# Which squares wait in DRAM: batches of plain-float32 matmuls every 32 steps, and every 48

## The chip, the core and the metric

The kernel runs on one core of a Trainium2 chip. The time is the device time of one execution in microseconds (us). Before the change it is 2217.09 us, the median of three runs (2216.71 to 2217.1). TensorE (PE) multiplies matrices, VectorE (DVE) and ScalarE (ACT) do elementwise work and take results out of PSUM, GpSimd (POOL) adds, and SyncE (SP) and ScalarE start DMAs.

## What is computed

A causal convolution of 7 softmaxed taps over 32,768 tokens of 192 features, then a two-layer network with a squared ReLU between:

```python
w = softmax(weight)                                  # 8 heads x 7 taps
x = einsum('hk,bskhg->bshg', w, unfolded(x))         # 32768 tokens x 192 features
h = x @ w_in                                         # 192 -> 2048
r = np.maximum(h, 0.0)
g = s * (r * r) + b
out = g @ w_out                                      # 2048 -> 192
```

Everything is float32. Most matmuls are done on pairs of a rounded part and a low part; that for the output's last 64 features is not.

## The kernel before, in words

Tokens lie along the free dimension. A **super** is 1024 tokens, `n` counts the 32 of them; a **block** is half of it (`j`, 512 tokens). The 2048 hidden features come in 8 pairs `p` of 128 + 128. A **step** is one (n, j, p): `first` (L528) makes 18 matmuls of the first layer into the PSUM tile `h`; ScalarE takes ReLU (L556) and square (L564) into a room `q`; VectorE rounds it to `qh` (L566) and takes the low part `ql` (L570); and two steps later `second` (L724) adds 12 matmuls into the accumulators of output features A, the first 128.

**Features B**, the last 64, aren't done in the step. From super 2 on (`OLD = 2`) the float32 squares are kept, and `second_B` (L743) multiplies them plainly, a whole block at a time: 64 matmuls on two PSUM banks, `acc1` and `acc2`. `banks()` hands these out of a pool with two of each name, so that block i of a batch writes the banks that block i - 2 had. `evict_B` takes the two banks out on ScalarE (L755, L756), adds them on GpSimd (L757), moves half of the rows by a DMA (L758), adds again (L761) and sends the result (L762).

The squares are kept in a ring of 12 rooms (`RING`), each of 1 MB for two steps, hence 24 steps. A batch is run at every 32nd step. Of a batch's four blocks, the first eight steps' squares have been sent to DRAM (`send`, L581, one DMA of 1 MB for every two steps, on SP's queue) and are called back (`call_back`, L591, four DMAs of 1 MB on ScalarE's queue) into rooms that the batch itself empties. So each batch has three **near** blocks, whose squares are in the ring, and one **far** block, done last. A room is given out when its last reader is done, so a call-back waits for a pair of matmul groups of the batch.

What sets the order: within PE, VectorE and ScalarE the instructions stay in the order in which the code is written (`in_order`), the DMAs that ScalarE starts among them. The convolution's taps (VectorE, L181 and L183, seven to a block's half) are handed out in pieces by `convolve(k)`: 7 pieces at the edge of a round, 5 during each block of a batch (`WINDOW`), none in the six steps from an edge on, then one or two in a step (`pace`). After the taps of the last 64 features, ScalarE rounds (L215) and starts the next input's load `xB` (L173). Each DMA counts its landing on one of eight shared counters, given out in turn; one that gets a counter again waits until the DMA that had it has landed.

Of the kernel before, what the change touches and what calls it, by code (L numbers as in the profile page):

```python
# [9 lines left out]
F32 = mybir.dt.float32  # L10
# [7 lines left out]
P = 128  # L18
BLK = 512
# [9 lines left out]

RING = 12  # L30

BATCH = 32

WINDOW = (5, 5, 5, 5)


GAP = 40

OLD = 2
# [9 lines left out]
def conv_attention_then_squared_relu_mlp(  # L49
# [23 lines left out]
    nc = tc.nc  # L73
    D, T = outT.shape
    NPAIR = weights64.shape[0]
# [28 lines left out]
    far = ctx.enter_context(tc.tile_pool(name="far", bufs=2, space=bass.MemoryType.DRAM))  # L104
    late = ctx.enter_context(tc.tile_pool(name="late", bufs=1))
    sumB = late.tile([P, 3 * DB], F32, name="sumB")
    ps_h = ctx.enter_context(tc.tile_pool(name="ps_h", bufs=2, space=bass.MemoryType.PSUM))
# [20 lines left out]
    @contextmanager  # L128
    def in_order(*engines):

        traced = nc.cur_bb.bb.instructions
        start = len(traced)
        yield
        for e in engines:
            mine = [i for i in traced[start:] if i.engine == e.engine]
            for before, i in zip(mine, mine[1:]):
                tc.add_manual_dep(
                    i,
                    before.name,
                    mybir.DependencyInfo(  # L140
                        mybir.DependencyClass.NoSync, mybir.DependencyReason.DATA
                    ),
                    reason="in_order",
                )
# [201 lines left out]
    def room_for(dtype):  # L346
        return act.tile([P, 2, 2, BLK], dtype, name="q")

    def flat(room):
        return room.rearrange("p a b c -> p (a b c)")  # L350

    places = [flat(room_for(I32)) for _ in range(3)]
    raw, rest = flat(room_for(I32)), flat(room_for(I32))
# [188 lines left out]
    two = [None]  # L542
# [16 lines left out]
    def squares(h, cast):  # L559
        return square(relu(h), cast)  # L560
# [8 lines left out]
    def lows(q, qh, ql):  # L569
        nc.vector.tensor_tensor(ql, q, qh.bitcast(F32), op=ALU.subtract)  # L570
        return qh, ql

    kept = {}

    away, double = {}, {}

    def send(n, p, queue=nc.sync):

        if p == 1:
            away[n] = far.tile([P, NPAIR // 2, 4 * BLK], F32, name="away")  # L580
        queue.dma_start(  # L581
            away[n][:, p // 2], double[n, p].rearrange("p a b c -> p (a b c)")
        )
        for k in (p - 1, p):
            del kept[n, 0, k]

    def call_back(n):

        for k in range(NPAIR // 2):
            room = room_for(F32)  # L590
            nc.scalar.dma_start(room.rearrange("p a b c -> p (a b c)"), away[n][:, k])  # L591
            for i in range(2):
                kept[n, 0, 2 * k + i] = room[:, i]
        del away[n]

    def put(n, j, p, pair):
        if n >= OLD:
            kept[n, j, p] = pair[0]
            if j == 0 and n % 2 == 0 and p % 2:
                double[n, p] = two[0]  # L600
        queue.append((n, j, p, *lows(*pair)))

    acc = {}
# [1 line left out]
    def banks():  # L605
        return [ps_o.tile([P, BLK], F32, name=f"acc{k}") for k in (1, 2)]
# [7 lines left out]
    room = ("oA", "oB", "oC", "oB2", "oA2", "oC2")  # L614

    def out_tile(name):
        return outs[:, room.index(name), :]
# [119 lines left out]
    def second_B(n, j, accs):  # L737

        for p in range(NPAIR):
            q = kept.pop((n, j, p))  # L740
            for r in (slice(0, HB), slice(HB, P)):
                for i in range(2):
                    nc.tensor.matmul(  # L743
                        accs[r.start // HB][i * DB : (i + 1) * DB], WB[r, p, i, :], q[r, i, :],
                        start=p == 0, stop=p == NPAIR - 1, skip_group_check=True,
                    )
        return accs

    def evict_B(n, j, accs, turn=0):

        t0 = n * SUP + j * BLK
        rooms = (("oB", "oB2", "oC"), ("oA", "oA2", "oC2"))[turn]
        o, o2, oC = (out_tile(name) for name in rooms)
        oC = oC[0:DB]
        nc.scalar.activation(o, accs[0], AF.Identity, scale=sb, bias=bias[:, 1:2])  # L755
        nc.scalar.activation(o2, accs[1], AF.Identity, scale=sb)  # L756
        nc.gpsimd.tensor_tensor(o, o, o2, op=ALU.add)  # L757
        nc.sync.dma_start(oC, o[DB:P])  # L758

        def rest():  # L760
            nc.gpsimd.tensor_tensor(oC, oC, o[0:DB], op=ALU.add)  # L761
            nc.sync.dma_start(outT[P:D, t0 : t0 + BLK], oC)  # L762

        return rest

    def last_B(n, j, accs):

        t0 = n * SUP + j * BLK
        oB = out_tile("oC2")[0:DB]
        nc.scalar.activation(  # L770
            oB, accs[0][DB:P], AF.Identity, scale=sb[DB:P], bias=bias[DB:P, 1:2]
        )
        for a in (accs[0][0:DB], accs[1][0:DB], accs[1][DB:P]):
            nc.vector.scalar_tensor_tensor(oB, a, sb[0:DB], oB, op0=ALU.mult, op1=ALU.add)
        nc.sync.dma_start(outT[P:D, t0 : t0 + BLK], oB)
# [20 lines left out]
    queue = []  # L796

    now = [0]
# [55 lines left out]
    def convolve(k):  # L854

        k += owed[0]
        owed[0] = 0
        while k > 0:
            said = next(stream, "over")
            if said in ("over", "gated"):  # L860
                return
            k -= 1
            burst[0] = k > 0
            if said == "tapped":
                owed[0] = k
                return
# [42 lines left out]

    def batch(k):  # L910

        n = OLD + 2 * k - 2
        rest = []
        for block, parts in zip(((n, 1), (n + 1, 0), (n + 1, 1), (n, 0)), WINDOW):
            a = second_B(*block, banks())
            convolve(parts)
            with in_order(nc.gpsimd, nc.sync):
                rest.append(evict_B(*block, a, len(rest) % 2))
                if len(rest) > 1:
                    rest[-2]()  # L920
            if block == (n + 1, 1):
                send(n + 2, 1, nc.scalar)
        convolve(0)
        rest[-1]()

    def pace(g):
        return 0 if g % BATCH < 6 else 2 if g % BATCH in (18, 20, 22) else 1

    steps = [(n, j, p) for n in range(NSUP) for j in range(2) for p in range(NPAIR)]

# [2 lines left out]
    def step(n, j, p):  # L933
        now[0] = 16 * n + 8 * j + p
        if p == 0:
            if j == 0:
                need(n, "A", 0)
                need(n, "B", 0)
                tok.pop(n - 1)
            else:  # L940
                need(n, "A", 1)
        g = now[0] - 16 * OLD
        h = first(n, j, p)
        edge = g % BATCH if g >= BATCH else BATCH
        if edge == 0:
            convolve(4)
            convolve(3)
            second(*queue.pop(0))
            waiting.append((n, j, p, h))
            return  # L950
        if edge == 1:
            second(*queue.pop(0))
            *at, before = waiting.pop()
            put(*at, squares(before, nc.vector.tensor_copy))
        put(n, j, p, squares(h, nc.scalar.copy if n == OLD and p % 2 else nc.vector.tensor_copy))
        if edge == 1:
            call_back(n - 2)
        if (n, j) == (1, 1):
            if p < NPAIR - 1:
                column_sums(p + 1)  # L960
            convolve(1)
        elif n <= OLD:
            convolve(3 if n == 1 else 2)
        else:
            convolve(pace(g))
        if (n, j, p) == (2, 0, 0):
            biases()
        elif n == 2 and p % 2 == 0 and unbiased:
            add_bias()
        if (n, j, p) == steps[-1]:  # L970
            call_back(n - 1)
            a = second_B(n - 1, 1, banks())
            evict_B(n - 1, 1, a)()
            for k, block in enumerate(((n, 0), (n - 1, 0), (n, 1))):
                h = ps_h.tile([P, 2, BLK], F32, name="h")
                a = second_B(*block, [h[:, k, :] for k in range(2)])
                if block == (n, 1):
                    last_B(*block, a)
                else:
                    evict_B(*block, a, 1 - k)()  # L980
            for item in queue:
                second(*item)
        while queue and len(queue) > LAG + (
            queue[0][2] == 0 and queue[0][0] <= OLD and queue[0][:2] not in ((1, 0), (OLD, 1))
        ):
            if (n, j, p) == steps[-1]:
                break
            second(*queue.pop(0))
        if edge == 1:
            batch(g // BATCH)  # L990
        sent = now[0] - 1
        if n >= OLD and sent % 32 < 8 and sent % 2 and edge != 2:
            send(sent // 16, sent % 8)

    with in_order(nc.vector, nc.scalar, nc.tensor):
        with in_order(nc.sync):
# [60 lines left out]
```

## Time and profile before

| What | us |
|---|---|
| Median of 3 runs | 2217.09 |
| The profiled execution | 2217.3 |
| Its span on the core | 2215.5 |
| Busy: PE, VectorE, ScalarE, GpSimd | 2210.2, 1610.6, 1331.4, 273.3 |
| Moved by DMA | 243.32 MB, mean 110 GB/s |
| From one batch to the next (410.50 to 547.19 in the chain) | 136.69 |

The span is the time from the first to the last instruction in the trace; 1.8 us of the execution lie around it. Fourteen batches of four blocks stand within the steps and one at the end, 60 blocks in all.

### The profile page before, as it was taken

To read this page: it belongs to the slowest core of one execution; us is meant where nothing else is said; L and a number is where in the kernel's file an instruction comes from. 1 tells how busy PE (TensorE), PEld (TensorE's weight loads), DVE (VectorE), ACT (ScalarE), POOL (GpSimd) and SP (SyncE) were. 2 spreads that over 40 slices of the span, in tenths; PEclk is the share of its full clock that TensorE was granted. 3 is DMA by queue.
4 is the path that set the end of the run, shared out by engine and by line. 5 is a ranking of instruction groups with operands and counts; after the bars stand their busy time and mean duration, and the time that the engine had idled before them with its cause. 6 is when DMAs were issued, how large, how long until landed. Compare 5 with 4: busy or idle time off the path is not lost.

```text
span 2215.5 us, 44748 instructions
## 1 busy us (share of the span) xinstructions
PE 2210.2 (100%) x19334; PEld 1611.2 (73%) x19334; DVE 1610.6 (73%) x1859; ACT 1331.4 (60%) x1449; POOL 273.3 (12%) x199
## 2 busy tenths in 40 slices
PE   9999999999999999999999999999999999999999
PEld 6788768587685876858778586785867858678585
DVE  8888777777777777777767777676776767767662
ACT  8759656466564665646556465564656646566463
POOL 0011020100202002020020201202011020110201
PEclk9999999999999999999999999999999999999999
DMA  5114151422515224152341523315233152421512
GB/s 167 39 32 161 55 199 53 162 91 65 193 49 162 100 77 173 54 172 82 104 144 54 174 86 117 126 53 191 73 132 107 54 195 68 146 94 53 205 30 103
DMA packets 63285, 243.32 MB, mean 110 GB/s; under 512 B 9648, under 2 KB 9904, under 8 KB 47728
## 3 DMA queue, kind: packets, MB, share of 16 engines
q1 hardware_dynamic: 43648, 138.98, 19.9%
q10 hardware_dynamic: 19440, 101.49, 12.9%
q8 instruction: 151, 2.47, 0.5%
q14 instruction: 46, 0.38, 0.1%
HBM read 94.55 MB, written 88.08 MB: 82 GB/s over the span
## 4 chain that ended last, share of the span: by engine, by line
PE 98%; DVE 1%; DMA 0%; ACT 0%; issue 0%; SPq 0%; DVEq 0%; ACTq 0%
PE h L528 47%; PE acc L724 29%; PE acc L743 18%; PE acc L670 2%; PE h L743 1%; PE acc L640 0%; PE acc L646 0%; DVE acc L183 0%; PE acc L648 0%; PE acc L647 0%; DVE ql L570 0%; PE acc L639 0%; DMA xA<-in_xA 0%; PE acc L642 0%; DVE q L308 0%; DVE q L322 0%
## 5 line engine op out<-in xcount | busy, mean ns | idle before, releaser
L556 ACT ACTIVATE q<-h 128x1024 f32<-128x1024 f32 x512 | 525.7, 1027 | 502.4 <-PE h L528 487.0
L566 DVE CAST qh<-q 128x1024 fp32r<-128x1024 f32 x482 | 334.1, 693 | 484.9 <-ACT q L564 481.6
L570 DVE TENSOR_TENSOR ql<-q,qh 128x1024 fp32r<-128x1024 f32 x498 | 623.8, 1253 | 56.4 <-ACT qh L566 4.9
L724 PE MATMUL acc<-qh,W 64*128 64x512 f32 x3816 | 588.0, 386 | 0.0
L564 ACT ACTIVATE q<-q 128x1024 f32<-128x1024 f32 x512 | 543.6, 1062 | 16.0
L528 PE MATMUL h<-wB,W 64*128 64x512 f32 x1536 | 430.1, 386 | 0.0
L528 PE MATMUL h<-sB,W 64*128 64x512 f32 x1536 | 430.1, 386 | 0.0
L528 PE MATMUL h<-sA,W 64*128 64x512 f32 x3024 | 426.9, 387 | 0.0
L528 PE MATMUL h<-wA,W 64*128 64x512 f32 x3024 | 425.2, 386 | 0.0
L724 PEld LDWEIGHTS acc<-qh,W 64*128 64x128 f32 x3816 | 357.4, 184 | 76.0 <-issue 0.8
L743 PE MATMUL acc<-q,WB 64*64 64x512 f32 x3648 | 394.9, 590 | 0.0
L724 PE MATMUL acc<-ql,W 64*128 64x512 f32 x1908 | 371.4, 386 | 0.0
L528 PEld LDWEIGHTS h<-sA,W 64*128 64x128 f32 x3024 | 282.2, 184 | 70.1 <-issue 11.4
L528 PEld LDWEIGHTS h<-wA,W 64*128 64x128 f32 x3024 | 283.6, 184 | 59.6
L183 DVE SCALAR_TENSOR_TENSOR acc<-xA,tap,acc 128x512 f32<-128x512 f32 x378 | 320.0, 847 | 7.6
L743 PEld LDWEIGHTS acc<-q,WB 64*64 64x64 f32 x3648 | 138.1, 133 | 248.9 <-issue 248.9
L528 PEld LDWEIGHTS h<-sB,W 64*128 64x128 f32 x1536 | 282.5, 184 | 30.9 <-issue 0.2
L528 PEld LDWEIGHTS h<-wB,W 64*128 64x128 f32 x1536 | 282.5, 184 | 30.1
L733 POOL TENSOR_TENSOR outs<-outs 128x512 f32<-128x512 f32 x59 | 95.4, 1617 | 1437.4 <-ACT outs L732 1437.4
L724 PEld LDWEIGHTS acc<-ql,W 64*128 64x128 f32 x1908 | 178.7, 184 | 37.7
L755 ACT ACTIVATE outs<-acc,bias,sb 128x512 f32<-128x512 f32 x57 | 44.4, 778 | 234.6 <-PE acc L743 163.9
L183 DVE SCALAR_TENSOR_TENSOR acc<-xB,tap,acc 128x512 f32<-128x512 f32 x186 | 140.0, 753 | 2.5
(145 smaller groups left out, 921.5 us busy)
## 6 DMA issues: line engine op xcount, KB each, us to landing
q<-away ACTq DMA_DIRECT2D x60, 1024.0 KB, 8.0
away<-q SPq DMA_DIRECT2D x46, 1024.0 KB, 4.2
wA<-sA SPq DMA_DIRECT2D x124, 256.0 KB, 3.7
wB<-sB SPq DMA_DIRECT2D x62, 256.0 KB, 4.0
outT<-outs SPq DMA_DIRECT2D x59, 256.0 KB, 2.0
away<-q ACTq DMA_DIRECT2D x14, 1024.0 KB, 4.6
xA<-in_xA ACTq DMA_DIRECT2D x23, 515.0 KB, 3.6
outT<-outs SPq DMA_DIRECT2D x62, 128.0 KB, 2.3
```

Source lines behind the costliest of these rows:

```text
L183: nc.vector.scalar_tensor_tensor(acc, src, w[:, k : k + 1], acc, op0=ALU.mult, op1=ALU.add)
L528: nc.tensor.matmul(h[:, i, :], w_in(w, p, chunk[0], rows), chunk[part], start=start, stop=stop)
L556: nc.scalar.activation(q, h, AF.Relu)
L564: nc.scalar.activation(q, q, AF.Square)
L566: cast(qh, q)
L570: nc.vector.tensor_tensor(ql, q, qh.bitcast(F32), op=ALU.subtract)
L670: nc.tensor.matmul(accs[to + 2 * i][0:cols], w(f, r), q[r, f % 2, :], start=start and f == 0, stop=stop and f == NF - 1,)
L724: nc.tensor.matmul(accs[i], w(f, r), q[r, f % 2, :], start=f == 0 and lo == 0, stop=f == ends[i] and lo == 2,)
L733: nc.gpsimd.tensor_tensor(o, o, o2, op=ALU.add)
L743: nc.tensor.matmul(accs[r.start // HB][i * DB : (i + 1) * DB], WB[r, p, i, :], q[r, i, :], start=p == 0, stop=p == NPAIR - 1, skip_group_c ...
L755: nc.scalar.activation(o, accs[0], AF.Identity, scale=sb, bias=bias[:, 1:2])
```

## The change

A round has 48 steps, and there are ten (`ROUNDS`). The first 24 steps of a round, three blocks, are sent to DRAM (`spilled`), where it was eight steps of 32. A batch has six blocks: three near, then three far (`blocks`). The call-back of the first far block is written at the round's edge as before, those of the second and the third after the first and the second block of the batch, between the evictions. Nine batches stand within the steps. After the last step `last_batch` does near, near, far, far, far, near. `pace` hands out two pieces in more of the steps.

```diff
-BATCH = 32
-WINDOW = (5, 5, 5, 5)
+ROUNDS = (48,) * 10
+WINDOW = 5
...
+    def spilled(at):
+        k, r = position(at)
+        return r < ROUNDS[k] - 2 * RING
+
+    def blocks(k):
+        z = (16 * OLD + sum(ROUNDS[: k + 1])) // NPAIR
+        y = z - 2 * RING // NPAIR
+        return list(range(y, z)), list(range(z - ROUNDS[k] // NPAIR, y))
...
     def batch(k):
-        n = OLD + 2 * k - 2
+        near, far_off = blocks(k)
         rest = []
-        for block, parts in zip(((n, 1), (n + 1, 0), (n + 1, 1), (n, 0)), WINDOW):
-            a = second_B(*block, banks())
-            convolve(parts)
+        for i, block in enumerate(near + far_off):
+            a = second_B(*place(block), banks())
+            convolve(WINDOW)
             with in_order(nc.gpsimd, nc.sync):
-                rest.append(evict_B(*block, a, len(rest) % 2))
-                if len(rest) > 1:
+                rest.append(evict_B(*place(block), a, i % 2))
+                if i:
                     rest[-2]()
-            if block == (n + 1, 1):
-                send(n + 2, 1, nc.scalar)
+            if i + 1 < len(far_off):
+                call_back(far_off[i + 1])
+            if i == max(2, len(far_off) - 1) and spilled(now[0]):
+                send(now[0], nc.scalar)
...
-    def pace(g):
-        return 0 if g % BATCH < 6 else 2 if g % BATCH in (18, 20, 22) else 1
+    def last_batch(k):
+        near, far_off = blocks(k)
+        if far_off:
+            call_back(far_off[0])
+        order = near[:2] + far_off + near[2:]
+        for i, block in enumerate(order):
+            if i:
+                h = ps_h.tile([P, 2, BLK], F32, name="h")
+                a = [h[:, k, :] for k in range(2)]
+            else:
+                a = banks()
+            a = second_B(*place(block), a)
+            if block == order[-1]:
+                last_B(*place(block), a)
+            else:
+                evict_B(*place(block), a, (len(order) - i) % 2)()
+            if i + 1 < len(far_off):
+                call_back(far_off[i + 1])
+
+    def pace(k, r):
+        if k and r < 6:
+            return 0
+        if r < 24:
+            return 2 if r > 7 and r % 5 in (1, 3) else 1
+        return 2 if r < 41 and (r % 2 == 0 or k + r % 3 == 0) else 1
...
-        if edge == 1:
-            call_back(n - 2)
+        if edge == 1 and blocks(k - 1)[1]:
+            call_back(blocks(k - 1)[1][0])
...
-        if n >= OLD and sent % 32 < 8 and sent % 2 and edge != 2:
-            send(sent // 16, sent % 8)
+        if now[0] - 1 in double and edge != 2:
+            send(now[0] - 1)
```

ScalarE's instructions of a batch before, in the order in which they stand, from the last of the four call-backs to the sending of the new round's first room (`L755`, `L756` an eviction of two banks, `L173` the load of `xB`; in brackets what a row waits for, `DMAHW` with a digit being one of the eight counters of landings):

```order
L591 DMA q<-away 128x2048 [waits DMAHW4_49,PE_49]
L755 ACTIVATE outs<-acc_3137,bias,sb 128x512
L756 ACTIVATE outs<-acc_3138,sb 128x512
L755 ACTIVATE outs<-acc_3180,bias,sb 128x512 [waits DMAHW0_49,PE_49,Pool_49]
L756 ACTIVATE outs<-acc_3181,sb 128x512 [waits PE_49]
L215 CAST sB<-acc 128x512 [waits DVE_49]
L173 DMA xB<-in_xB 128x518 [waits DMAHW7_49,DMAHW6_49]
L755 ACTIVATE outs<-acc_3221,bias,sb 128x512 [waits DMAHW5_49,PE_49,Pool_49]
L756 ACTIVATE outs<-acc_3222,sb 128x512 [waits PE_49,Activation_49]
L581 DMA away<-q 128x2048 [waits DMAHW3_49]
```

The same engine in a batch of the change, from the load of `xB` (now L172) to that sending (now L584); `L594` are the four call-backs of the third far block, `L776` and `L777` evictions, of the second and then the third near block. Ahead of these stand, in this order, the first far block's four call-backs, the first near block's eviction, the second far block's four call-backs and the rounding (L214):

```order
L172 DMA xB<-in_xB 128x518 [waits DMAHW4_49]
L776 ACTIVATE outs<-acc_3857,bias,sb 128x512 [waits Pool_49]
L777 ACTIVATE outs<-acc_3858,sb 128x512
L594 DMA q<-away 128x2048 [waits DMAHW6_49,PE_49]
L594 DMA q<-away 128x2048 [waits DMAHW2_49,PE_49]
L594 DMA q<-away 128x2048 [waits DMAHW3_49,PE_49]
L594 DMA q<-away 128x2048 [waits DMAHW4_49,PE_49]
L776 ACTIVATE outs<-acc_3918,bias,sb 128x512 [waits DMAHW0_49,Pool_49]
L777 ACTIVATE outs<-acc_3919,sb 128x512 [waits Activation_49]
L584 DMA away<-q 128x2048 [waits DMAHW5_49]
```

The third near block's eviction (banks 3918 and 3919) stood behind a load and two evictions; now four call-backs stand ahead of it, and the last of them waits for counter 4, the one that the load of `xB` uses. The same holds in each of the nine batches.

On PE before, the end of a batch's third block (banks 3221, 3222) and the start of its fourth and last:

```order
L743 MATMUL acc_3222<-q,WB 64x512 x2
L743 MATMUL acc_3279<-q,WB 64x512 [waits DMAHW1_49,Activation_49]
L743 MATMUL acc_3279<-q,WB 64x512
L743 MATMUL acc_3280<-q,WB 64x512 [waits Activation_49]
L743 MATMUL acc_3280<-q,WB 64x512
L743 MATMUL acc_3279<-q,WB 64x512 x2
```

On PE in the change, the end of the fourth block (the first far one, banks 3963 and 3964) and the start of the fifth, the second far one:

```order
L764 MATMUL acc_3964<-q,WB 64x512 x2
L764 MATMUL acc_4011<-q,WB 64x512 [waits DMAHW7_49,PE_49,Activation_49]
L764 MATMUL acc_4011<-q,WB 64x512
L764 MATMUL acc_4012<-q,WB 64x512 [waits PE_49,Activation_49]
L764 MATMUL acc_4012<-q,WB 64x512
L764 MATMUL acc_4011<-q,WB 64x512 x2
```

The fourth block waited for the second block's eviction; the fifth block, which is new, waits for a call-back's landing and for the eviction of the third near block (banks 3918 and 3919), whose banks it takes over.

More of the change, by code (lines that the diff above doesn't have):

```diff
@@ L575, in conv_attention_then_squared_relu_mlp, with place, send, call_back @@
     away, double = {}, {}
-    def send(n, p, queue=nc.sync):
+    def place(block):
+        return block // 2, block % 2
+    def send(at, queue=nc.sync):
+        block, p = at // NPAIR, at % NPAIR
         if p == 1:
-            away[n] = far.tile([P, NPAIR // 2, 4 * BLK], F32, name="away")
+            away[block] = far.tile([P, NPAIR // 2, 4 * BLK], F32, name="away")
         queue.dma_start(
-            away[n][:, p // 2], double[n, p].rearrange("p a b c -> p (a b c)")
+            away[block][:, p // 2], double.pop(at).rearrange("p a b c -> p (a b c)")
         )
         for k in (p - 1, p):
-            del kept[n, 0, k]
-    def call_back(n):
+            del kept[*place(block), k]
+    def call_back(block):
         for k in range(NPAIR // 2):
             room = room_for(F32)
-            nc.scalar.dma_start(room.rearrange("p a b c -> p (a b c)"), away[n][:, k])
+            nc.scalar.dma_start(room.rearrange("p a b c -> p (a b c)"), away[block][:, k])
             for i in range(2):
-                kept[n, 0, 2 * k + i] = room[:, i]
-        del away[n]
+                kept[*place(block), 2 * k + i] = room[:, i]
+        del away[block]
+    def spilled(at):
[5 more added lines that the diff above has]
+        return list(range(y, z)), list(range(z - ROUNDS[k] // NPAIR, y))
+    def position(at):
+        k, r = 0, at - 16 * OLD
+        while r >= ROUNDS[k]:
+            r -= ROUNDS[k]
+            k += 1
+        return k, r
     def put(n, j, p, pair):
@@ L598, in put @@
             kept[n, j, p] = pair[0]
-            if j == 0 and n % 2 == 0 and p % 2:
-                double[n, p] = two[0]
+            at = 16 * n + 8 * j + p
+            if p % 2 and spilled(at):
+                double[at] = two[0]
         queue.append((n, j, p, *lows(*pair)))
@@ L941, in step @@
                 need(n, "A", 1)
-        g = now[0] - 16 * OLD
+        k, r = position(now[0]) if n >= OLD else (0, 0)
         h = first(n, j, p)
-        edge = g % BATCH if g >= BATCH else BATCH
+        edge = r if k else None
         if edge == 0:
@@ L964, in step @@
         else:
-            convolve(pace(g))
+            convolve(pace(k, r))
         if (n, j, p) == (2, 0, 0):
@@ L970, in step @@
         if (n, j, p) == steps[-1]:
[L971 to L980, printed above, removed]
+            last_batch(k)
             for item in queue:
@@ L989, in step @@
         if edge == 1:
-            batch(g // BATCH)
-        sent = now[0] - 1
-        if n >= OLD and sent % 32 < 8 and sent % 2 and edge != 2:
-            send(sent // 16, sent % 8)
+            batch(k - 1)
+        if now[0] - 1 in double and edge != 2:
+            send(now[0] - 1)
     with in_order(nc.vector, nc.scalar, nc.tensor):
```

## The prediction

> **What bounds the kernel now.** I read the shares of busy time first, then the chain that ended last, then one batch in order of time.
>
> ```profile
> PE 2210.2 (100%) x19334; PEld 1611.2 (73%) x19334; DVE 1610.6 (73%) x1859; ACT 1331.4 (60%) x1449; POOL 273.3 (12%) x199
> PE 98%; DVE 1%; DMA 0%; ACT 0%; issue 0%; SPq 0%; DVEq 0%; ACTq 0%
> 270.41 2.04 PE h L528 x18
> 272.45 1.36 PE acc L724 x12
> 273.81 27.63 PE acc L743 x256
> 301.43 2.30 PE h L528 x18
> ...
> 410.50 27.63 PE acc L743 x256
> 438.13 2.30 PE h L528 x18
> 547.19 27.63 PE acc L743 x256
> ```
>
> PE never waits: a step is 2.04 + 1.36 = 3.40 us, a batch 27.63, so a block takes 27.63 / 4 = 6.91 and a pair (a room's two groups) 1.73. The first layer's matmuls right behind a batch take 2.30 instead of 2.04. That closes the account: 32 x 3.40 + 27.63 + 0.26 = 136.69, which is 547.19 - 410.50. All that a rarer batch can save is the 0.26 of each batch that goes: the blocks are 60 before and after, the steps 480.
>
> **What is removed.** Fourteen batches within the steps become nine: 5 x 0.26 = **1.3 us less**. This is also the most that any edit here can gain, since nothing else on PE becomes less.
>
> **What is added and hidden.** Sixty rooms more go out in the steps, on SP's queue, and the taps are spread anew.
>
> ```profile
> q<-away ACTq DMA_DIRECT2D x60, 1024.0 KB, 8.0
> away<-q SPq DMA_DIRECT2D x46, 1024.0 KB, 4.2
> L566 DVE CAST qh<-q 128x1024 fp32r<-128x1024 f32 x482 | 334.1, 693 | 484.9 <-ACT q L564 481.6
> L570 DVE TENSOR_TENSOR ql<-q,qh 128x1024 fp32r<-128x1024 f32 x498 | 623.8, 1253 | 56.4 <-ACT qh L566 4.9
> L183 DVE SCALAR_TENSOR_TENSOR acc<-xA,tap,acc 128x512 f32<-128x512 f32 x378 | 320.0, 847 | 7.6
> ```
>
> A room is sent every second step, 6.80 us, and lands in 4.2: the steps cover it. VectorE has 0.693 + 1.253 = 1.95 a step, with two taps 3.64, which is 0.24 over the step; but a step with one tap has 0.60 to spare, doubles and singles mostly alternate, and PE uses `ql` only two steps later. So 0; without that slack, 16 double steps x 10 rounds x 0.24 = 38 us. A gain is excluded by the busy PE.
>
> **What is added and not hidden: twelve call-backs in one batch.** Now one batch before, on ScalarE, with the time to landing of two DMAs, and the DMA engines in the same microseconds.
>
> ```profile
> 415.56 4.07 ACTq L591 DMA_DIRECT2D q<-away  x4
> 419.68 0.78 ACT L755 ACTIVATE outs<-acc,bias,sb 128x512 f32<-128x512 f32 x1 [3.12 <-PE acc L743]
> 420.36 0.68 ACT L756 ACTIVATE outs<-acc,sb 128x512 f32<-128x512 f32 x1
> 421.73 0.34 ACTq L173 DMA_DIRECT2D xB<-in_xB  x1
> L591 ACTq DMA_DIRECT2D q<-away x1: 326/326/326, 419.3 to 419.3; - x1
> DMA to landing us min/median/max: 12.4/12.4/12.4
> L173 ACTq DMA_DIRECT2D xB<-in_xB x1: 340/340/340, 421.7 to 421.7; - x1
> DMA to landing us min/median/max: 12.0/12.0/12.0
> ...
> 418.00:420.00 2.00, 2.00 (x24) 0.69 (x20) 1.96 (x3) 0.32 (x1) 0.00 (x0) 1.00 1.03 434
> 420.00:422.00 2.00, 2.00 (x24) 0.69 (x20) 1.93 (x4) 1.37 (x3) 0.88 (x1) 1.00 1.01 426
> 422.00:424.00 2.00, 2.00 (x24) 0.77 (x20) 2.00 (x3) 0.29 (x1) 0.77 (x1) 1.00 1.01 418
> ```
>
> Three things are read here. (1) The DMA engines are full (share 1.01 to 1.03) at 418 to 434 GB/s, so a room of 1024 KB, 1.049 MB, takes 2.42 to 2.51 us, I take 2.45; the batch empties a room every 1.73. (2) The first block ended at 410.50 + 6.91 = 417.41, yet its eviction begins at 419.68, right behind the fourth call-back's start (419.31): a call-back that waits holds up what stands behind it on ScalarE. (3) `xB`, queued behind the four call-backs, lands at 421.73 + 12.0 = 433.7, which is 23.2 after the batch's start. In another batch (start 1640.74, row of the chain) it lands at 1651.97 + 10.8, 22.0 after the start:
>
> ```profile
> 1640.74 27.63 PE acc L743 x256
> ...
> L173 ACTq DMA_DIRECT2D xB<-in_xB x1: 339/339/339, 1652.0 to 1652.0; - x1
> DMA to landing us min/median/max: 10.8/10.8/10.8
> ```
>
> In the change eight call-backs stand ahead of `xB`. Their rooms come free by 2.25 blocks (15.5 us), earlier than the full DMA engines can take them, so `xB` comes 4 x 2.45 = 9.8 later, with 0.3 for an output of 128 KB that now falls ahead of it: 32.1 to 33.3 after the start, I take **32.7**. The twelfth call-back waits for just that landing, by its counter (the rows of ScalarE above). Behind it stands the third near block's eviction, and the fifth block's matmuls wait for that one (the rows of PE), due at 4 x 6.91 = 27.6. Behind the landing come 0.37 for the start of the DMA (419.31 to 419.68) and 0.68 + 0.68 for the two evictions, with the semaphores about 1.8: PE goes on at 34.5. A stall of **6.9 us** a batch (6.3 to 7.5 by the two batches).
>
> The wait itself is new, so its bounds: below, the last far block's data alone, worked out as a rival (1.8); above, if the delay of the 12.4 us call-back (5.0 more than 3 x 2.45) came a second time, 6.9 + 5.0 = 12. I take 6.9, nearest to the rows of `xB`. Also queued behind the waiting call-back are the new room's sending, which nobody needs before the ring comes round, and the first far block's eviction, whose banks the sixth block needs a block later. The twelfth room, started at 32.7 behind three others, lands by 32.7 + 4 x 2.45 = 42.5; it is then due at 39.7 + 6.9 = 46.6. On SP's queue the swaps of `sB` and the evictions' inner DMAs also come later; their readers are 16 steps and two blocks away.
>
> **The clock behind the stall.** The first matmuls of the run, and its end, in order of time and by windows (the last but two columns is the granted clock):
>
> ```profile
> 0.99 3.78 PE L393 MATMUL acc<-q 128*128 128x512 f32 x6 [0.99 <-POOL xA L167]
> 4.56 6.75 PE L257 MATMUL acc<-xB,q 128*128 128x512 f32 x14
> 13.36 3.17 PE L257 MATMUL acc<-xA,q 128*128 128x512 f32 x7
> ...
> 2209.96 1.60 PE acc L785 x6
> ...
> 2211.70:2214.10 2.40, 0.00 (x0) 0.00 (x0) 0.88 (x2) 0.00 (x0) 0.00 (x0) 1.00 0.43 137
> 2214.20:2215.50 1.30, 0.00 (x0) 0.00 (x0) 0.00 (x0) 0.00 (x0) 0.00 (x0) 0.50 0.00 0
> ```
>
> PE's last matmul ends at 2211.56, and from 2214.2 the granted clock is 0.50: some 2.6 us of idleness were enough. 6.9 us are more. What coming back costs, the run's start shows: seven matmuls of 512 columns take 3.17 at 13.36, 0.45 each; the first six, as much as four of these (two of 512 columns, four of 256), take 3.78 instead of 1.8, the next fourteen 6.75 instead of 6.3: 2.4 lost. I take **2.3 us** a batch (0 if the clock stays, 3.4 if the slow time is half as long again).
>
> The Trainium skill (TensorE: Matmul & The Clock Gate, section "What's actually happening") says that the array goes to half rate after an idle window of about 3.4 us and back after a busy one. The trace's end agrees (0.50); by the page's figure the loss would be an estimated 1.7 a batch, and the sum 2297.
>
> The Trainium skill (DMA: Bandwidth & Descriptors, "Where 436 GB/s comes from") says that transfers between HBM and SBUF are held to about 358 GB/s by the HBM side. The rows show 434, and the measurement decides; by the page's figure a room would take an estimated 2.93, and nine batches 35 us more: 2337.
>
> **The last batch.** There the call-backs start earlier, and nothing but small outputs runs beside them.
>
> ```profile
> 2179.35 7.03 PE acc L743 x64
> ...
> 2181.29 5.48 ACTq L591 DMA_DIRECT2D q<-away  x4
> ...
> L591 ACTq DMA_DIRECT2D q<-away x1: 326/326/326, 2186.4 to 2186.4; - x1
> DMA to landing us min/median/max: 9.8/9.8/9.8
> ```
>
> The fourth lands at 2196.2, 16.9 after the start; eight more take 19.6, so the twelfth lands at 36.5. Its pair is due at 4.75 blocks, 32.8: **3.7 us** (0 to 6), in waits too short for the clock.
>
> **The sum**, against the profiled execution's 2217.3 (the median, 2217.09, is 0.2 less): 2217.3 - 1.3 + 9 x (6.9 + 2.3) + 3.7 = 2302.5. I predict **2302 us**.
>
> **Rivals.**
> - *The clock stays.* Only the stall: 2302 - 9 x 2.3 = 2281. For it: the half clock is seen only at the two ends of the run.
> - *Late data alone.* The wait for `xB` doesn't bind, say because `xB` overtakes. Then the twelfth room decides: the fourth landed at 419.31 + 12.4, 21.2 after the start, in batches with less contention three earlier; eight more at 2.45, 0.6 for `xB` and some 0.9 of outputs give 39.3 to 42.3, due at 5.75 blocks, 39.7. 0 to 2.6 a batch, 1.8 if most are like the one shown: 2217.3 - 1.3 + 16 + 3.7 = 2236 (2217 to 2256, the upper end with half of the clock's loss).
> - *Not slower: the DMA engines keep up.* If `xB` lands by 27.6 - 1.8 = 25.8 after the start and the twelfth room by 39.7, no batch waits: 2217.3 - 1.3 = 2216. The first call-back starts at 415.56, 5.1 after the start, and eight rooms take 19.6: 24.7. So it holds if latency and all other transfers together cost under 1.1 us. Against it: behind only four, 5.1 + 9.8 = 14.9, `xB` lands at 22.0 to 23.2.
> - *Later still.* The contention comes with each far block: 12 + 3 a batch give 2217.3 - 1.3 + 135 + 6 = 2357 at the most.
>
> **How the numbers follow.** The forecast 0.56 (from 6.3 + 1.2 to 7.5 + 3.4 a batch with the last batch's ends: 2283 to 2320), the clock stays 0.14, late data alone 0.12, not slower 0.07, later still 0.11. From 2260 to 2335 lie the first two, and the near parts of late data and of later still: about 0.8. 0.2%, 4.4 us, is about what a measurement of this kernel can tell from no change. A gain is 1.3 at most, so faster has 0.02; same 0.06; slower 0.92.
>
> **What would show it.** Right: in the changed profile PE idle once in each of the nine batches, at the fifth block, some 7 us, released by the eviction on ScalarE, which sits behind the call-backs; the granted clock 0.50 behind it; DMA near 430 GB/s for 30 us; nine gaps of about 0.26 where 14 stood. Wrong: the idle time at the sixth block and released by a DMA (late data), clock 1.00 throughout (the clock stays), PE at 100% (they keep up), or idle PE in the steps (VectorE's double taps).

## The result, and the profile after

The kernel with batches every 48 steps takes **2312.97 us** (2310.22 to 2315.4), the kernel before 2216.99 beside it: a ratio of 1.0432 (95% interval 1.0419 to 1.0446). It is 96.0 us slower, with the same 60 blocks and the same 480 steps. The profiled execution took 2313.28, its span is 2311.5, its mean granted clock 0.982.

From the page of the changed kernel, busy time by engine and the shares of the chain that ended last:

```profile
PE 2235.6 (97%) x19334; PEld 1654.5 (72%) x19334; DVE 1571.8 (68%) x1859; ACT 1331.6 (58%) x1449; POOL 263.5 (11%) x199
PE 89%; DMA 8%; DVE 1%; ACT 1%; ACTq 0%; issue 0%; POOL 0%; SPq 0%; DVEq 0%; POOLq 0%
```

PE executes as many matmuls as before, yet is busy for 25.4 us more (2235.6 against 2210.2): some ran slower. And the chain, which was PE almost alone, now goes through DMAs for 8% of the span. The waits of the changed kernel (total us, times, longest) say where:

```profile
PE acc L764 <- ACT outs L776: 66.5, 9, 7.9
ACT outs L776 <- DMA xB<-in_xB: 112.8, 7, 16.6
```

Nine waits, one for each batch within the steps, 7.4 us each: PE waits for an eviction, and the eviction for the landing of `xB`. (In seven of the nine; in the other two the profile names a call-back, but there too `xB` landed 0.5 ahead of the eviction.) One batch, on PE and then on ScalarE, in order of time (start, duration, instruction, in brackets the idle time before it and what ended it; the view of PE ends at 806, inside the last two blocks):

```profile
758.76 27.70 PE L764 MATMUL acc<-q,WB 64*64 64x512 f32 x256
793.69 12.84 PE L764 MATMUL acc<-q,WB 64*64 64x512 f32 x94 [7.24 <-ACT outs L776]
```

```profile
763.89 4.07 ACTq L594 DMA_DIRECT2D q<-away  x4
...
769.35 5.48 ACTq L594 DMA_DIRECT2D q<-away  x4
...
774.89 0.42 ACTq L172 DMA_DIRECT2D xB<-in_xB  x1
...
778.13 14.62 ACTq L594 DMA_DIRECT2D q<-away  x4
792.86 0.78 ACT L776 ACTIVATE outs<-acc,bias,sb 128x512 f32<-128x512 f32 x1 [16.11 <-DMA xB<-in_xB]
```

Four blocks run without a gap (27.70), then PE stands still until 0.8 us after the eviction at 792.86 began. That eviction is the third near block's; its banks were full at 758.76 + 3 x 6.91 = 779.5, and it stood 13 us behind the last four call-backs. The chain through the same batch shows what they waited for:

```profile
774.89 17.46 DMA xB<-in_xB
...
792.43 0.33 ACTq L594
...
793.69 16.57 PE acc L764 x128
```

The landing of `xB` at 792.35, 33.6 after the batch's start, lets the twelfth call-back go, and that lets the eviction go. The last two blocks, 128 matmuls, then take 16.57 instead of 2 x 6.91 = 13.82. The same stretch by windows (the last three columns are the granted clock, the DMA engines' share and their GB/s; the first figure behind the window's length is PE's busy time):

```profile
786.00:788.00 2.00, 0.45 (x8) 0.00 (x0) 1.74 (x3) 0.00 (x0) 0.00 (x0) 1.00 0.97 298
...
790.00:792.00 2.00, 0.00 (x0) 0.00 (x0) 0.00 (x0) 0.00 (x0) 0.00 (x0) 0.90 1.08 443
792.00:794.00 2.00, 0.31 (x2) 0.29 (x4) 0.00 (x0) 1.14 (x2) 0.00 (x0) 0.50 1.01 426
794.00:796.00 2.00, 2.00 (x10) 1.00 (x10) 0.00 (x0) 0.22 (x1) 1.64 (x2) 0.50 1.02 430
796.00:798.00 2.00, 2.00 (x14) 1.17 (x10) 0.00 (x0) 1.12 (x2) 0.84 (x1) 0.50 1.00 418
798.00:800.00 2.00, 2.00 (x22) 1.25 (x18) 0.00 (x0) 0.23 (x1) 1.27 (x1) 0.90 1.01 417
```

A mean of 0.90 in 790 to 792 means that the clock halved at 791.6; by the 0.90 of the last row it was whole again at 798.4. From 793.69 on, 4.7 us of work ran at half clock: 10 and 14 matmuls in 2 us where 24 belong. That is where most of PE's additional busy time comes from.

All nine batches together, from the first and the last start in the chain:

```profile
327.92 15.65 PE acc L764 x144
...
2048.53 15.65 PE acc L764 x144
```

A round takes (2048.53 - 327.92) / 8 = 215.08. Its work is 48 x 3.40 + 6 x 6.91 + 0.26 = 204.9. So a batch costs **10.2 us** more than its blocks; nine make 92. The last batch, on PE and in the chain:

```profile
2280.53 1.95 PE L764 MATMUL h<-q,WB 64*64 64x512 f32 x16 [0.49 <-DMA q<-away]
...
2294.18 8.81 PE L764 MATMUL h<-q,WB 64*64 64x512 f32 x80 [0.88 <-DMA q<-away]
```

```profile
2255.84 7.07 PE acc L764 x64
...
2275.56 6.60 DMA outs<-outs
2282.20 11.94 DMA q<-away
2294.18 8.81 PE h L764 x80
2302.99 2.96 PE acc L745 x24
```

It takes 2302.99 - 2255.84 = 47.15 instead of 6 x 6.91 = 41.45, **5.7 us** more: six waits of 4.4 together, and at each restart 0.2 (a pair takes 1.95 alone and 1.73 in the flow). Its twelfth call-back, too, was held up by a landing that it does not need: a transfer of half an output, 6.60 us, on the counter that it wanted.

### The profile page after: what moved, and what is told of

Same layout as the page of the kernel before. It is cut to its first block, busy times and chain, and to the rows that moved or that the text cites. A ratio compares the mean times of both kernels' runs of the same rounds, so it can differ in the third digit from the quotient of the medians.

```text
span 2311.5 us, 45007 instructions
## 1 busy us (share of the span) xinstructions
PE 2235.6 (97%) x19334; PEld 1654.5 (72%) x19334; DVE 1571.8 (68%) x1859; ACT 1331.6 (58%) x1449; POOL 263.5 (11%) x199
## 4 chain that ended last, share of the span: by engine, by line
PE 89%; DMA 8%; DVE 1%; ACT 1%; ACTq 0%; issue 0%; POOL 0%; SPq 0%; DVEq 0%; POOLq 0%
PE h L527 45%; PE acc L745 28%; PE acc L764 13%; DMA xB<-in_xB 5%; DMA q<-away 2%; PE acc L691 1%; DMA outs<-outs 1%; PE h L764 0%; ACT outs L776 0%; PE acc L661 0%; PE acc L667 0%; PE acc L669 0%; DVE acc L182 0%; PE acc L668 0%; ACTq L594 0%; DVE ql L569 0%
## 5 line engine op out<-in xcount | busy, mean ns | idle before, releaser
L764 PE MATMUL acc<-q,WB 64*64 64x512 f32 x3520 | 406.4, 616 | 66.5 <-ACT outs L776 66.5
L764 PEld LDWEIGHTS acc<-q,WB 64*64 64x64 f32 x3520 | 176.8, 139 | 290.8 <-issue 211.4
L182 DVE SCALAR_TENSOR_TENSOR acc<-xA,tap,acc 128x512 f32<-128x512 f32 x378 | 309.2, 818 | 6.6
L776 ACT ACTIVATE outs<-acc,bias,sb 128x512 f32<-128x512 f32 x55 | 42.8, 777 | 299.0 <-DMA xB<-in_xB 112.8
```

Of the source, the lines that this page charges most:

```text
L182: nc.vector.scalar_tensor_tensor(acc, src, w[:, k : k + 1], acc, op0=ALU.mult, op1=ALU.add)
L764: nc.tensor.matmul(accs[r.start // HB][i * DB : (i + 1) * DB], WB[r, p, i, :], q[r, i, :], start=p == 0, stop=p == NPAIR - 1, skip_group_c ...
```

## The experiments

Each is an edit of the changed kernel. Where a ratio stands, it is to the kernel before, which took 2216.7 to 2216.8 beside them.

**The eviction ahead of the third far block's call-backs.**

```diff
-            if i + 1 < len(far_off):
-                call_back(far_off[i + 1])
+            if i in (0, 2):
+                call_back(far_off[1 if i == 0 else 2])
```

> The third far block's call-backs are written behind the third near block's eviction, nothing else moves. If the idle time at the fifth block comes from that eviction standing behind call-backs on ScalarE, it goes from 7.4 us to under 0.5; what is left is late data at the sixth block, 4 us a batch in gaps under 2 us, the granted clock stays 1.00, and the time is about 2257 us (2245 to 2270). If the data of the far blocks sets the idle time whatever the order, the time stays at 2313.

Measured 2290.64 us (2286.55 to 2296.82), ratio 1.0339 (1.0321 to 1.0356). PE in one batch:

```profile
539.90 32.85 PE L764 MATMUL acc<-q,WB 64*64 64x512 f32 x304
573.17 1.95 PE L764 MATMUL acc<-q,WB 64*64 64x512 f32 x16 [0.42 <-DMA q<-away]
577.12 7.64 PE L764 MATMUL acc<-q,WB 64*64 64x512 f32 x48 [2.00 <-ACT outs L776]
587.03 1.95 PE L764 MATMUL acc<-q,WB 64*64 64x512 f32 x16 [2.27 <-DMA q<-away]
```

The time lies outside what was expected. The wait at the fifth block is gone, as the theory says, but it comes back one block later: the four call-backs now stand ahead of the first far block's eviction, whose banks the sixth block needs (2.00), and the last room lands late (2.27). Rounds take 212.5, so 7.6 a batch are left, not the 4 expected. So the eviction behind the call-backs is one part of the matter, 22 of the 96 us; the other is that the call-backs themselves can't start. In this batch the tenth starts at 573.97, right behind the landing of `xB` (573.95).

**Half the bytes.** Each call-back fetches the first half of a room, and both groups multiply that half; the kernel leaves out the other half of the far blocks' squares.

```diff
-            nc.scalar.dma_start(room.rearrange("p a b c -> p (a b c)"), away[block][:, k])
+            nc.scalar.dma_start(
+                room.rearrange("p a b c -> p (a b c)")[:, 0 : 2 * BLK], away[block][:, k, 0 : 2 * BLK]
+            )
...
-                kept[*place(block), 2 * k + i] = room[:, i]
+                kept[*place(block), 2 * k + i] = room[:, 0]
```

> Each call-back brings only the first half of a room, and the matmuls read that half twice, so the far blocks' other squares are left out. The order and the number of instructions are the same. If bytes set the landing of xB, it comes 8 x 1.2 = 10 us earlier, at some 24 us after a batch's start, no batch waits and the time is about 2216 (2214 to 2222). If a fixed cost of each call-back or of the waits sets it, the time stays near 2313.

Measured 2215.17 us in one run, clock 1.000. Its page:

```profile
PE 2207.9 (100%) x19334; PEld 1611.5 (73%) x19334; DVE 1581.5 (71%) x1859; ACT 1331.6 (60%) x1449; POOL 271.8 (12%) x199
```

The order on ScalarE, the counters and the number of DMAs are those of the changed kernel; with half the bytes no batch makes PE wait, and `xB` lands 21.6 after the start of the first one. So the late landings come from the time that the bytes take, and everything else in the change (60 more sends, the taps in pairs, five batches fewer) costs nothing that shows: 2217.3 - 1.3 = 2216.0 was the sum for that.

**Idle time filled with matmuls.** Fourteen instructions that the result does not use, 6.28 us, ahead of the fifth block.

```diff
+            if i == 4:
+                idle_h = ps_h.tile([P, 2, BLK], F32, name="h")
+                for m in range(7):
+                    nc.tensor.matmul(
+                        idle_h[:, m % 2, :], sumA[:, 0, 0:P], sumA.rearrange("p a b -> p (a b)"),
+                        start=True, stop=True,
+                    )
```

> Seven plain float32 matmuls of 512 columns, whose result nobody reads, stand ahead of the fifth block's matmuls: some 6.3 us of work in the idle time. If the half clock behind the idle time costs 2.5 us a batch on its own, the granted clock stays 1.00 in the batches and the time falls by 9 x 2.5 to about 2290 (2283 to 2297), with the eviction as late as before. If the clock costs nothing here, it stays at 2313 or rises.

Measured 2295.41 us (2294.29 to 2298.5), ratio 1.0356 (1.0342 to 1.037), clock 1.000. One batch:

```profile
568.34 6.28 PE L939 MATMUL h<-sumA 128*128 128x512 f32 x14
575.84 14.53 PE L764 MATMUL acc<-q,WB 64*64 64x512 f32 x128 [1.22 <-ACT outs L776]
```

The stall stays (the fifth block begins 35.1 after the batch's start), and the clock no longer drops. The last two blocks take 14.53, in all nine batches; in the changed kernel they take 16.39 to 16.92, 16.68 on average. So the clock costs 16.68 - 14.53 = 2.15 a batch, and 14.53 - 13.82 = 0.7 has nothing to do with it: the second of the two banks is taken out 0.68 later than the first, and PE needs both. The whole gain, 17.6 us, is 1.95 for each of nine batches.

**Rounds of 40 steps**, two far blocks a batch instead of three.

```diff
-ROUNDS = (48,) * 10
+ROUNDS = (40,) * 12
```

> Twelve rounds of 40 steps, each with three near and two far blocks: eight call-backs a batch, none of them ahead of the third near block's eviction but the eight that are freed by then. If call-backs ahead of that eviction make the idle time, there is none at the fifth block beyond 0.5 us of late data; 11 batches within the steps instead of 14 save 0.8 us and the last batch costs some 2: about 2219 (2215 to 2224). If any second far block costs its data's lateness, 11 x 3 us more: about 2250.

Measured 2221.48 us (2220.38 to 2222.81), ratio 1.0021 (1.0012 to 1.0029), clock 1.000. From its waits:

```profile
PE acc L764 <- DMA q<-away: 2.2, 5, 0.7
```

No eviction holds up PE any more: with two far blocks a batch the stall isn't there. It was the third that brought it.

**The third far block's call-backs on SP's queue.**

```diff
-    def call_back(block):
+    def call_back(block, queue=nc.scalar):
...
-            nc.scalar.dma_start(room.rearrange("p a b c -> p (a b c)"), away[block][:, k])
+            queue.dma_start(room.rearrange("p a b c -> p (a b c)"), away[block][:, k])
...
-                call_back(far_off[i + 1])
+                call_back(far_off[i + 1], nc.sync if i else nc.scalar)
```

> The third far block's call-backs are started on SP's queue, not ScalarE's; nothing else moves. If what is queued behind them on ScalarE makes the idle time, it goes at the fifth block, and late data at the sixth remains as in the run with the eviction first: 2285 us (2265 to 2300). If the call-backs' order or number on the DMA engines makes it, the fifth block goes on waiting and the time stays at 2313.

Measured 2296.43 us in one run, at the upper end of what was expected. Its waits:

```profile
PE acc L764 <- DMA q<-away: 52.2, 43, 2.3
PE acc L764 <- ACT outs L776: 1.0, 3, 0.4
```

The evictions are free, and the data is late instead: 43 short waits. On a queue of its own the ninth call-back starts early and shares the DMA engines with rooms that are due before it: in the batch from 541.81 it lands 27.6 after the start (36.0 in the batch shown of the changed kernel), and the eighth 35.4 instead of 33.1. Another queue gave no bandwidth here.

**The taps of the first four blocks given out at the fifth.** The rounding of `sB`, its swap (two transfers of 256 KB from `sB` to `wB`) and the load of `xB` follow the taps; with the taps later, they come behind the call-backs.

```diff
-            convolve(WINDOW)
+            for _ in range(5 if i == 4 else i > 4):
+                convolve(WINDOW)
```

> The taps of a batch's first four blocks are handed out at the fifth, so that the load of xB and the swap of sB stand behind all call-backs and the twelfth call-back waits on its counter for the sixth one, not for xB. If the idle time is the eviction behind that landing, there is none at the fifth block, and with 0.9 MB less ahead of the twelfth room the late data are 0 to 3 us a batch: 2217.3 - 1.3 + 9 x 2 + 5.7 = 2240 (2221 to 2255). If twelve rooms in one batch are late whatever runs beside them, 7.6 us a batch remain as with the eviction first: 2290.

Measured **2237.23 us** (2236.51 to 2238.7), ratio 1.0093 (1.008 to 1.0107), clock 1.000. ScalarE and PE in one batch (start 535.09):

```profile
560.28 0.78 ACT L776 ACTIVATE outs<-acc,bias,sb 128x512 f32<-128x512 f32 x1 [7.71 <-DMA q<-away]
...
564.40 0.34 ACTq L172 DMA_DIRECT2D xB<-in_xB  x1
```

```profile
535.09 38.00 PE L764 MATMUL acc<-q,WB 64*64 64x512 f32 x352
573.68 1.95 PE L764 MATMUL acc<-q,WB 64*64 64x512 f32 x16 [0.59 <-DMA q<-away]
```

This takes away 76 of the 96 us, though all the call-backs stand ahead of the eviction as before: the order on ScalarE is that of the changed kernel but for `xB` and the rounding. With these and the swap out of the way the counters come round otherwise, and each late call-back waits for an earlier landing. The tenth starts 21.8 after the batch's start, behind the fifth room's landing, and the twelfth 24.8, behind the sixth's; in the changed kernel's batch they started at 29.9 and 33.7, behind the seventh's and that of `xB`. So the eviction begins 25.2 after the start instead of 34.1. What is left is late data, 1.7 a batch. This settles the cause: with the same order of call-backs and eviction, the stall goes when the call-backs' waits for landings end earlier.

**The last batch with its near blocks first.**

```diff
-        order = near[:2] + far_off + near[2:]
+        order = near + far_off
```

> Only the last batch changes: near, near, near, far, far, far, not near, near, far, far, far, near. The far rooms are then due a block later. If the last batch's 5.7 us are late data, nearly all of them go: about 2308 us (2306 to 2311). If they come from the evictions, 2313 remains.

Measured 2310.01 us in one run: 3 us less than the median, but only 0.2 below the lowest of the changed kernel's runs. In the traces the stretch from the last batch's start to the end takes 2.0 less (53.65 against 55.66). PE's waits in the last batch shrink to one of 0.35; the nine others stay (7.0 to 7.9).

**Both, the taps even later** (all of them at the sixth block).

```diff
-            convolve(WINDOW)
+            for _ in range(6 if i == 5 else i > 5):
+                convolve(WINDOW)
...
-        order = near[:2] + far_off + near[2:]
+        order = near + far_off
```

> Both: all taps of a batch are handed out at its sixth block, and the last batch has the order near, near, near, far, far, far. xB and the swap of sB then run behind the last room. If bytes beside the twelve rooms are what makes them late, 0 to 1 us a batch is left: 2217.3 - 1.3 + 9 x 0.5 + 0.5 = 2221 (2215 to 2229), and VectorE is late by 2 us behind a batch without PE waiting for it. If it makes PE wait, 9 x 2 us more. If twelve rooms are late by themselves, 2285.

Measured 2285.41 us (2283.78 to 2287.23), ratio 1.031 (1.0296 to 1.0324): the theory fell, by 64 us. Its waits, and VectorE behind one batch:

```profile
PE acc L745 <- DVE qh L565: 26.7, 9, 4.8
DVE sB L207 <- ACT sB L214: 247.3, 9, 28.7
```

```profile
580.40 1.42 DVE L207 TENSOR_TENSOR sB<-acc,sB 128x512 fp32r<-128x512 f32 x1 [28.02 <-ACT sB L214]
581.75 5.58 DVE L182 SCALAR_TENSOR_TENSOR acc<-xA,tap,acc 128x512 f32<-128x512 f32 x6
...
588.81 6.49 DVE L182 SCALAR_TENSOR_TENSOR acc<-xA,tap,acc 128x512 f32<-128x512 f32 x6
595.21 0.69 DVE L565 CAST qh<-q 128x1024 fp32r<-128x1024 f32 x1
```

VectorE stood idle for 28 us, since the rounding that it needs now stands behind the evictions on ScalarE; then 13 taps in a row stand ahead of the first `qh` of the next steps, and PE waits for that instead, with the clock at half again. The wait went from one in-order engine to the next. That the time meets the 2285 set down for "twelve rooms are late by themselves" is chance: for rooms the batches within the steps wait 9.0 in all, and the eighth room of the batch from 539.83 lands 30.0 after its start.

**Both, the taps at the fifth block** (the edit of the taps as in the sixth experiment, the order as above).

> The taps of the first four blocks given out at the fifth, and in the last batch the three near blocks ahead of the far ones. Theory (the two effects lie in different places and add up): the taps alone measured 2237.2, the order of the last batch took its waits from about 5 us to 0.35, so 2237.2 - 4.7 = 2232.5 (2230 to 2235), with the nine batches still at about 1.7 us each over the sum of their blocks. Rival (the last batch also gets its late taps in the way): 2237 or more.

Measured 2235.76 us (2234.78 to 2236.8), ratio 1.0086 (1.007 to 1.0101): 1.5 less than with the taps alone, not 4.7, and the two ranges overlap. PE's waits of the last batch, five with the taps alone, became one of 0.88 and PE finishes 3.6 earlier, but the end is now set by another chain:

```profile
2210.93 6.69 DMA outs<-outs
...
2220.28 2.21 DMA outs<-outs
...
2226.29 0.78 ACT outs L791
```

These are evictions of the far blocks that take turns at the same tiles, each through a small transfer that takes 6.69 beside the call-backs and 2.21 without. Off PE's path before, they end last now. The order alone has the same rows at its end, which is why it gained 2 to 3 and not 5.

**Rounds of 40 with both edits**, the taps given out at the fourth of five blocks.

```diff
-ROUNDS = (48,) * 10
+ROUNDS = (40,) * 12
...
-            convolve(WINDOW)
+            for _ in range(4 if i == 3 else i > 3):
+                convolve(WINDOW)
...
-        order = near[:2] + far_off + near[2:]
+        order = near + far_off
```

> Twelve rounds of 40 steps (two far blocks a batch), the taps given out at the fourth of the five blocks, and in the last batch the near blocks first. Theory (what rounds of 40 lose are waits for data that comes late beside the load of xB and the swap of sB, 0.3 to 0.7 in the batches that have them, and 1.3 in the last batch; later taps move that load behind the call-backs): 11 batches instead of 14 within the steps save 3 x 0.26 = 0.8, so 2217.1 - 0.8 = 2216.3 (2215 to 2218), at best 0.04% less than the kernel before. Rival (the late taps hold up VectorE behind the batch, as all of them at the sixth block did in rounds of 48): 4 to 8 us in each batch that has the taps, 2225 or more.

Measured **2215.41 us** (2215.22 to 2216.19), ratio 0.9994 (0.9985 to 1.0003): no difference from the kernel before that can be told. Its chain:

```profile
1837.29 34.49 PE acc L764 x320
...
2008.05 34.49 PE acc L764 x320
```

A batch is one piece again, 5 x 6.91 = 34.5 without a gap. A round is 170.76, and 40 x 3.40 + 34.5 + 0.26 = 170.8. That is all there was to gain: three batches fewer, 0.8 us.

## Why the prediction was right

The forecast was 2302 us, by a stall at the fifth block with a loss of clock behind it. The time is 2313, and the trace and the experiments show that mechanism.

- **What is removed, 1.3, and what is hidden, 0.** Right: with half the bytes the time is 2215.17, where these two steps give 2216.0. PE waits for VectorE nowhere in the steps.
- **The stall, 6.9 a batch.** Right in place and releaser, and nearly in size: 7.4 on average, 6.9 to 7.9, and 0.7 more behind it (next point). `xB` lands 33.6 after the start of the batch shown (33.3 to 34.3 in the nine), where 32.7 was taken. That it came so near is in part luck. The four more rooms ahead of `xB` were taken at 4 x 2.45 = 9.8, and in the batch shown they took 13.8 (the fourth landed at 778.06, the eighth at 791.87). Against that, the fourth room landed 19.3 after the start and `xB` 0.5 behind the eighth, 19.8 together, where 22.6 was carried over from the batches before, with 0.3 for an output. The two errors nearly cancel. One nuance: the eleventh call-back, too, started only at 791.9, right behind the eighth's landing (774.5 + 17.4), 0.5 ahead of the twelfth. The landing of `xB` was the last of several that held the queue, and without its wait alone the stall would by this be half a microsecond shorter. What ended it was the move of `xB`, the rounding and the swap together, which let all the call-backs start earlier; which of the three counts most was not tried apart.
- **The restart.** The working's 1.8 behind the landing counts the evictions of both banks, and that was right: in the batch shown the second one ends 1.9 behind the landing. PE goes on when the first bank is out, though, and the second comes 0.68 later; so 0.7 of the loss stands not in the idle time but in the last two blocks, at full clock. To compare with the 6.9 are 7.4 + 0.7 = 8.1, and the difference is nearly all the later landing of `xB`. With the clock, 7.4 + 0.7 + 2.15 make the 10.2 of a batch.
- **The clock, 2.3 a batch.** Right: 2.15 by the run with matmuls in the gap, 4.7 / 2 = 2.35 by the windows. The half clock at the end of the run was the only row of the granted clock that gave it away. The Trainium skill (TensorE: Matmul & The Clock Gate, "What's actually happening") says that the window which the chip watches is free-running and some 3.4 us long; the 6.8 us at half clock here are two of them, and the 10.2 in six of the nine batches are three, so the trace agrees with the length (that the window is free-running no run here shows), and the estimate of 1.7, which took one such window, was a little low. On the idle time that it takes, which the prediction gives from the same section of the Trainium skill as about 3.4 us, the trace at the end of the run before does not agree: 2.6 us were enough there, so the prediction's "agrees" holds for the half rate alone.
- **The last batch, 3.7.** Under-sized: 5.7. The twelfth call-back was taken to start as soon as the DMA engines could serve it; it waited for a counter behind a half output's transfer of 6.60 and landed 38.4 after the start, not 36.5. And each of the six restarts costs 0.2.
- **The sum.** Nine times 10.2 instead of 9.2, mostly by the later landing of `xB`, and 2.0 in the last batch: 2302.5 + 9 + 2 = 2313.5, against the profiled 2313.28.
- **The rivals.** "The clock stays" fell by the windows. "Not slower" is what half the bytes gives (2215.17). "Late data alone" is what the kernel becomes when `xB` no longer stands ahead: 2237.23, where 2236 was worked out. With `xB` left where it is and only the eviction moved, late data and what comes with it cost 7.6 a batch, which that rival had not priced: the call-backs wait for landings of others before they can wait for bandwidth. "Later still" had the contention right in kind (in the batch shown the sixth, seventh and eighth room landed 4.0, 4.3 and 3.3 us behind the one before, not 2.45) and fell in size.

## What to carry to other kernels

Where an engine with work of its own starts DMAs in order, write down for each start which landing it waits for, and what stands behind it: that work is late by the slowest of these landings, even one whose data nobody needs yet. Where counters are given out in turn, moving a DMA also changes which landing each later one waits for. Before more data is sent through DRAM, compare its arrival with its use, here 2.45 us a room against 1.73; the difference adds up over the batch (twelve rooms late, eight just in time), and it is better to hold the batch below the point where the cover ends. And ask first what the change can gain: here 0.26 for each batch that goes, so that a single wait undoes it.

## What the runs showed of the hardware

- Beside the loads of 1 MB, small transfers take three to four times as long (a half output 6.6 to 9.2 in the batch shown and the last one, against 2.21 where no load runs beside it). For a while the full DMA engines also move less: 298 to 358 GB/s in the windows from 780 to 790 of the batch shown, 417 to 443 from 790 to 800, at a share near 1 in both. The swap of `sB`, a half output and an output are under way in the slow stretch. A half output is under way from 795.65 to 802.57 as well, at 417 and 418 GB/s in the windows from 796, so the swap is the likelier cause. With the taps at the fifth block, and so the swap later, the eighth room lands 30.0 after the start instead of 33.1. But the swap's second transfer lands at 787.97, and 788 to 790 is still slow (335); no run here changed one of these alone, and the cause stays open.
- Less idleness than expected halves the clock. With the eviction moved ahead, the batch shown above had waits of 0.42 and 2.00 at the sixth block; by windows:

```profile
578.00:580.00 2.00, 2.00 (x16) 0.80 (x12) 0.00 (x0) 0.00 (x0) 2.00 (x2) 0.57 1.01 426
580.00:582.00 2.00, 2.00 (x12) 0.51 (x11) 0.00 (x0) 1.35 (x2) 0.47 (x2) 0.57 1.06 401
```

Two rows at 0.57 are half clock for 3.4 us, after no more than 2.4 us of idleness. Not every such wait did it: that kernel's clock halved six times between its first batch and its last, with three to five waits in each of nine batches.
